# Local and pooled attention before an MLP: value chunks loaded in order and attended as they land

## The chip, the cores and the metric

One core of a Trainium2 chip runs the whole program. The metric is device time in microseconds (us). The kernel before takes 307.57 us, the median of three runs (307.49, 307.57, 308.89). Engines are named as the profile names them: PE (TensorE, matrix multiplication; PEld is its weight load), ACT (ScalarE), DVE (VectorE), POOL (GpSimd) and SP (SyncE, which here only issues loads and stores).

## What is computed

```python
def _attn_ref(q, k, v):
    # q, k, v: 8 batches, 8 heads, 576 tokens, head size 64
    q_d, k_d, v_d = means of q, k, v over groups of 4 tokens
    out_up = repeat(softmax(scale * q_d @ k_d.T) @ v_d, 4)
    mask = abs(i - j) < 4
    out_local = softmax(where(mask, scale * q @ k.T, -1e9)) @ v
    return out_up + out_local

def _moe_ref(x, w_in, w_out):
    # x: 4608 tokens x 512, w_in: 512 x 2048, w_out: 2048 x 512
    h = x @ w_in
    g = h * (1.0 / (1.0 + exp(-1.702 * h)))
    return g @ w_out
```

The attention's output, heads side by side, is the x of the second part. All inputs and the output are float32; the kernel computes its products in bfloat16.

## The kernel before, in words

**Two parts.** Attention runs batch by batch, the MLP by groups of 512 tokens (`n_groups` is 9, `TG` 512). A group's first product (`mm1`, L753, matmuls by `hps_mm` L738) goes through ScalarE's Silu (L749) into `gT`; the second (`mm2`, L770, matmuls at L808) is scaled and stored (L783 to L794). Within group g the attention of batch g+1 is placed between matmuls of `mm1` and `mm2` by a list of positions (`POS`, `POS_G`, L838, L839): a position counts matmul steps, and positions from 16 on are steps of `mm2`. `VDP_0` (L840) is the position at which batch 1's values are pooled by PE.

**Order by hand.** No scheduler orders the instructions: each engine runs its own in the order of the program's text. Only semaphores join engines, and an instruction that waits holds back everything behind it on its engine.

**Batch 0** has no MLP work to hide under; lines 847 to 938 are its order.

- Loads of k, q and w go through POOL's queue and are cast to bfloat16 on the way (`load_1` L183, `load_vb` L214, `load_w_in` L237, `load_w_out` L246). A "quad" (qd) is four heads: q and k come in one load per quad, 128 partitions by 1152 values. POOL's queue holds at most eight loads that have not landed.
- Values come in five chunks of 128 rows that overlap (`KSTART`, steps of 114 tokens), each chunk in two loads of 64 partitions. Before, chunk 4 of batch 0 is asked for first of all, as float32 through SP and ACT (`load_v` at L847, L203), and cast by ACT (`prep_v`, L865, L325). Chunks 0 to 3 come through POOL's queue behind k and q.
- DVE transposes k and q (L261) and sums them over four tokens (`reduce_qk` L304; POOL does the second quad's q by `pool_qk`, L315 and L319). PE makes the masked local scores (`scores` L419: L381 and L394) and the pooled ones (`scores_d` L428: L411); ACT takes their exponentials (L477, L483) into `es` and `ed`.
- `prep_vd_pe` (L351) sums values over four tokens on PE with a selection matrix (L362), in three blocks: kc 0 reads chunks 0 and 1, kc 1 reads 1, 2 and 3, kc 2 reads 3 and 4. ACT copies the blocks to `vd` (L371).
- `av_local0` (L493, L499) multiplies local weights by values for a pair of heads (hp, 0 to 3), `av_down0` (L507, L513 and L522) the pooled ones. Both write to the pair's accumulator `o[hp]`, in which one column of each block of 65 is the sum of weights. Columns 0 to 3 of the blocks belong to chunks 0 to 3, 4 and 5 to chunk 4 and the pooled part, 6 to the pooled part.
- `normalise0` (L537) divides on DVE: a reciprocal (L541) and products (L544, L549), in the parts "a" (blocks 0 to 3), "b" (4 to 6) or both.
- `transp_sum` (L557, L564 and L575; called by `turned`) turns a pair's result so that the model dimension is on partitions, and ACT copies it to `xT` (L587, L591).
- `part` is group 0's first product, started on each quarter of the model dimension as its `xT` comes.
- `warm` (L603, matmuls at L606) issues matmuls that nobody reads; with `z=wf` they are float32 and take two passes.

Before, PE waits until chunks 0 to 3 are there, pools blocks kc 0 and 1, does the local part of pairs 0 and 1 with all five chunks, and DVE normalises part "a".

Of the kernel before, what the change touches and what calls it, by code (L numbers as in the profile page):

```python
# [19 lines left out]
def kernel(  # L20
# [9 lines left out]
    nc = tc.nc  # L30
    B, H, S, D = q.shape
    SD = S // 4
    HP = H // 2
    NQ = H // 4
# [158 lines left out]
        load_1("k", k, kf, b, qd)  # L193
        load_1("q", q, qf, b, qd)

    def load_v(b, gate=None, chunks=range(5), queues=(nc.sync, nc.sync)):
        t = ldp.tile([128, 5, H, D], FP32, name="vf", tag="vf")
        vf[b] = t
        if gate is not None:
            gate(t[0:1, 0, 0, 0:1])  # L200
        for i in chunks:
            for par in range(2):
                queues[par].dma_start(  # L203
                    out=t[64 * par : 64 * par + 64, i],
                    in_=bass.AP(
                        tensor=v.tensor,
                        offset=v[b, 0].offset + (114 * i + KSTART[par]) * D,
                        ap=[[D, 64], [S * D, H], [1, D]],
                    ),
                )  # L210
# [95 lines left out]
                axis=mybir.AxisListType.X, op=ALU.add,  # L306
            )

    def pool_qk(b, qd, names="kq"):
        for name, src in (("k", kT), ("q", qT)):  # L310
            if name not in names:
                continue
            sv = src[b, qd].rearrange("p (j f) a -> p j f a", f=4)
            t1 = work.tile([128, SD, 2, 2], FP32, name="pq", tag="pq")
            nc.gpsimd.tensor_tensor(  # L315
                out=t1, in0=sv[:, :, 0:2, :], in1=sv[:, :, 2:4, :], op=ALU.add
            )
            dst = kdT[qd][:, 0:SD, :] if name == "k" else new_qdT(b, qd)
            nc.gpsimd.tensor_tensor(  # L319
                out=dst, in0=t1[:, :, 0, :], in1=t1[:, :, 1, :], op=ALU.add  # L320
            )
# [26 lines left out]
    def flat(p):  # L348
        return p.rearrange("p x n -> p (x n)")

    def prep_vd_pe(b, pv, kcs=range(3), between=None):  # L351
        n = HP
        vb, vd = vbs[b % 2], vds[b % 2]
        for kc, iis in ((0, (0, 1)), (1, (1, 2, 3)), (2, (3, 4))):
            if kc not in kcs:
                continue
            c0 = 256 * (kc - kcs[0])
            if between and kc == 1:
                between()
            for i in iis:  # L360
                for j in range(2):
                    nc.tensor.matmul(  # L362
                        pv[64 * j : 64 * j + 64, c0 : c0 + D * n],
                        lhsT=psel[:, PSEL.index((i, kc)), :],
                        rhs=sub(
                            vb[:, i], 65 * (2 * j if b else j), (4 * 65, NQ), (65 * (1 if b else 2), 2), (1, D)
                        ),
                        start=(i == iis[0]), stop=(i == iis[-1]),
                        tile_position=(0, 64 * j),
                    )  # L370
        nc.scalar.copy(  # L371
            out=vd[:, kcs[0] : kcs[-1] + 1, :, 0:D],
            in_=pv[:, 0 : 256 * len(kcs)].rearrange(
                "p (k h d) -> p k h d", k=len(kcs), h=HP
            ),
        )


    def bar_others(sp):
# [157 lines left out]
    def normalise0(o, y, u, parts="ab"):  # L537
        yl, yd, rc = y
        ov = o[:, :, 0:455].rearrange("p x (c e) -> p x c e", e=65)
        c0, c1 = {"a": (0, 4), "b": (4, 7), "ab": (0, 7)}[parts]  # L540
        nc.vector.reciprocal(rc[:, :, c0:c1], ov[:, :, c0:c1, 64:65])  # L541
        if "b" in parts:
            st = 2 - u
            nc.vector.tensor_tensor(  # L544
                out=yd.rearrange("p s x d -> p x s d"), in0=ov[:, :, 4 + u : 7 : st, 0:D],
                in1=rc[:, :, 4 + u : 7 : st].to_broadcast([128, 2, 2, D]), op=ALU.mult,
            )
            c1 = 6
        nc.vector.tensor_tensor(  # L549
            out=yl[:, :, c0:c1], in0=ov[:, :, c0:c1, 0:D],  # L550
            in1=rc[:, :, c0:c1].to_broadcast([128, 2, c1 - c0, D]), op=ALU.mult,
        )
# [217 lines left out]
    def mm2(g, gT, steps):  # L770
# [29 lines left out]
        for t, ffc, run in order:  # L800
            if g == n_groups - 1 and t == 3:
                continue
            for f in steps.get(n, ()):
                f()
            n += 1
            if ffc % run == 0:
                ops[t] = pm_tile()
            nc.tensor.matmul(  # L808
                ops[t],
                lhsT=gT[:, ffc, t * 128 : (t + 1) * 128],  # L810
                rhs=w_out_bf[:, ffc, :],
                start=(ffc % run == 0), stop=(ffc % run == run - 1),
            )
            if ffc == n_ffc - 1:
                store(t, ops[t], 0, d_model, nc.scalar, nc.sync, part.get(t))
            elif ffc % run == run - 1:
                keep(t, ops[t])

# [17 lines left out]
            f()  # L836

    POS = [13, 16, 34, 44, 58, 65]  # L838
    POS_G = {0: [16, 18, 29, 42, 56, 65], 1: [13, 16, 35, 44, 58, 65]}  # L839
    VDP_0 = 34  # L840

    o, y, x = {}, {}, {}

    def after(src, eng):
        return lambda t: eng.tensor_copy(out=t, in_=src)

    load_v(0, chunks=[4], queues=(nc.sync, nc.scalar))  # L847
    nc.scalar.preload_act_table_set("exp_and_others")
    load_qk(0, 0)
    load_1("k", k, kf, 0, 1)  # L850
# [1 line left out]
    load_1("q", q, qf, 0, 1)  # L852
    iota_psel()
    fill()
    for i in range(4):
        load_vb(0, i)
    load_w_in(0, 512)
    warm(3, z=wf)
    warm(5, 256)
    make_off()  # L860
    make_ident(di)
    make_psel()
    make_bias()
    end_psel()
    prep_v(0, nc.scalar, 4)  # L865
    prep_1("k", 0, 0)
    prep_1("q", 0, 0)
    sp = scores(0, 0, PA[0:2])
# [2 lines left out]
    prep_1("k", 0, 1)  # L871
    prep_1("q", 0, 1)
    reduce_qk(0, 0, "q")
    pool_qk(0, 1, "q")
    reduce_qk(0, 1, "k")
    for c in range(1, 4):
        load_w_in(512 * c, 512)
    for qd in range(NQ):
        load_qk(1, qd)
    load_w_out(0)  # L880
    load_w_out(4)
    warm(2, z=wf)
    sp = scores(0, 1, PA[0:2])
    exp_local(1, sp)
# [1 line left out]
    for hp in range(4):  # L886
        o[hp] = PA[hp % 3]
        y[hp] = y_tiles0()
    warm(1, z=wf)
    prep_vd_pe(0, PM[0], range(0, 2))  # L890
    for hp in range(2):
        av_local0(hp, o[hp], range(5))
        normalise0(o[hp], y[hp], hp % 2, "a")
    prep_vd_pe(0, PM[1], range(2, 3))
    exp_down(1, scores_d(0, 1, PA[2]))
    nc.scalar.preload_act_table_set("silu_and_others")
    for hp in range(2):
        if hp == 1:
            warm(1, t=PM[0])
        av_down0(hp, o[hp])  # L900
        normalise0(o[hp], y[hp], hp % 2, "b")

    gT0 = new_gT()
    acc = PM + [PA[n][:, u, :] for n in (1, 2, 0) for u in range(2)]
# [4 lines left out]
            for ffc in ffcs:  # L909
                hps_mm(0, ffc, dmc, acc[ffc])  # L910

    def av_whole0(hp):
        av_local0(hp, o[hp], range(5))
        av_down0(hp, o[hp])
        normalise0(o[hp], y[hp], hp % 2)

    def turned(hp, n):
        x = PM if n is None else [PA[n][:, u, :] for u in range(2)]
        transp_sum(y[hp], x)
        copy_x(0, hp, PM if n is None else PA[n][:, :, 0:288])  # L920

    av_whole0(2)
    warm(1, t=PM[0])
    turned(0, None)
    av_whole0(3)
    turned(1, 1)
    part((0, 1), 0)
    part((0, 1), 1)
# [11 lines left out]
    for g in range(n_groups):  # L940
        b = g + 1
        if g == 0:
            load_vb(1, 0)
            load_vb(1, 1)
            prep_qk(1, 0)
            pool_qk(1, 0)
            prep_qk(1, 1)
            load_vb(1, 2)
            load_vb(1, 3)
            load_vb(1, 4)  # L950
            load_w_out(8)
            load_w_out(12, 2)
            load_w_out(14, 2)
            reduce_qk(1, 1, "q")
            reduce_qk(1, 1, "k")
            for qd in range(NQ):
                load_qk(2, qd)
            nc.gpsimd.memset(v4[32:64], 0.0)
            for x, c in ((0, 1.0), (1, 4.0)):
                nc.vector.memset(ones[:, x, :], c)  # L960
            load_v(2, gate=after(w_out_bf[0:1, 14, 0:1], nc.gpsimd))
            load_v4(2)
        elif b == 2:
            for p in (0, 64):
                nc.vector.tensor_copy(out=mask[p : p + 64, 1], in_=mask[64 - p : 128 - p, 0])
            prep_qk(b, 0)
            pool_qk(b, 0)
            prep_qk(b, 1)
            keep_odd(b, 1)
            swap_even("k", b, 1)  # L970
            swap_odd("k", b, 1)
            reduce_qk(b, 1, "k")
            swap_even("q", b, 1)
            swap_odd("q", b, 1)
            load_qk(b + 1, 0)
            prep_vx(b)
            load_v(b + 1)
            prep_v4(b, nc.gpsimd, (0,))
            pool_qk(b, 1, "q")
            prep_v4(b, nc.gpsimd, (1, 2))  # L980
            load_qk(b + 1, 1)
        elif b < B:
            if b + 1 < B:
                load_v(b + 1)
            swap_odd("k", b, 0)
            swap_even("q", b, 0)
            swap_odd("q", b, 0)
            if b > 3:
                prep_v4(b, nc.gpsimd, (0, 1))
            pool_qk(b, 0)  # L990
            prep_qk(b, 1)
            keep_odd(b, 1)
            for name in "kq":
                swap_even(name, b, 1)
                swap_odd(name, b, 1)
            prep_v4(b, nc.gpsimd, (2,) if b > 3 else (0, 1))
            pool_qk(b, 1)
            if b == 3:
                prep_v4(b, nc.gpsimd, (2,))
# [57 lines left out]
```

## Time and profile before

| What | Value |
|---|---|
| Median of three runs | 307.57 us |
| Profiled execution, its own time | 308.58 us |
| Its span, first to last instruction | 306.8 us |
| Time around the span | 1.78 us |
| Instructions | 8494 |
| Mean granted PE clock | 0.999 |
| DMA | 40.01 MB, mean 130 GB/s |
| POOL's queue (q0) | 18352 packets, 14.81 MB |
| Instruction queue (q8) | 28 packets, 0.46 MB |

How to read it: the page gives each engine's busy time; the busy times by stretch say in which part of the span an engine is full; the chain that ended last is followed back from the last instruction, so that its rows are the work that set the time; the timeline lists instructions in order with the idle time before each and what ended it ("<-DMA" is a load, "<-issue" is a wait for nothing that the profile shows). Besides, the trace records when each load's semaphore was raised, by each of the 16 DMA engines that share a load, and when the blocks of program text on the instruction queue were moved.

### The profile page before, as it was taken

How to read it: one execution, taken by the hardware profiler on the slowest of the kernel's cores; microseconds unless marked ns; L12 is line 12 of the kernel's file. 1: busy time of each engine (PE TensorE's matmuls, PEld its weight loads, DVE VectorE, ACT ScalarE, POOL GpSimd, SP SyncE). 2: the span in 40 equal slices, each digit the busy share in tenths (PEclk: the TensorE clock that was granted, in tenths of full speed). 3: DMA queues.
4: the chain of work that ended last, by engine and by line, in shares of the span. 5: the costliest groups of instructions: out<-in, count | busy, mean ns of one | idle time of the engine just before them, and what ended most of it. 6: DMA issues, size and time to landing. Idle time of an engine off the chain costs nothing.

```text
span 306.8 us, 8494 instructions
## 1 busy us (share of the span) xinstructions
PE 298.0 (97%) x3551; PEld 147.8 (48%) x3551; DVE 187.1 (61%) x354; ACT 212.9 (69%) x351; POOL 178.9 (58%) x217
## 2 busy tenths in 40 slices
PE   7879999999999999999999999999999999999995
PEld 3455455444554455445544554455444544444444
DVE  6865523966999689886897689777975430000000
ACT  5545887867887788668966896689769876226511
POOL 8855792599698968976797669845983300000000
PEclk9999999999999999999999999999999999999999
DMA  7999999999899969826973598425101110010012
GB/s 147 152 203 209 173 132 213 177 221 215 177 230 188 188 133 226 219 46 113 232 211 66 88 218 232 84 77 150 72 0 37 36 71 0 34 71 34 0 68 71
DMA packets 64662, 40.01 MB, mean 130 GB/s; under 512 B 44656, under 2 KB 56048, under 8 KB 64624
## 3 DMA queue, kind: packets, MB, share of 16 engines
q0 software_dynamic: 18352, 14.81, 35.8%
q1 hardware_dynamic: 45600, 24.46, 32.3%
q8 instruction: 28, 0.46, 0.6%
q10 hardware_dynamic: 672, 0.20, 0.3%
q14 instruction: 10, 0.08, 0.1%
HBM read 44.83 MB, written 9.44 MB: 177 GB/s over the span
## 4 chain that ended last, share of the span: by engine, by line
PE 93%; DMA 4%; issue 1%; POOL 1%; DVE 0%; ACT 0%; POOLq 0%; DVEq 0%
PE pm L808 40%; PE pm L738 36%; PE pa L681 5%; PE pa L738 5%; DMA qb<-in_q_dram 2%; DMA vb<-in_v_dram 2%; PE pa L449 2%; PE pm L824 1%; PE pa L458 1%; PE pa L394 1%; PE pa L411 0%; POOL kb L183 0%; PE pa L513 0%; PE pa L362 0%; PE pa L499 0%
## 5 line engine op out<-in xcount | busy, mean ns | idle before, releaser
L808 PE MATMUL pm<-w_out_bf,gT 128*128 128x512 bf16 x560 | 126.2, 379 | 0.0
L738 PE MATMUL pm<-xT,w_in_bf 128*128 128x512 bf16 x512 | 119.2, 379 | 0.3 <-ACT xT L591 0.3
L749 ACT ACTIVATE gT<-pm 128x512 bf16<-128x512 f32 x128 | 76.3, 598 | 42.7 <-PE pm L738 42.7
L738 PEld LDWEIGHTS <-w_in_bf 128*128 128x128 bf16 x576 | 55.6, 98 | 67.2 <-issue 0.6
L808 PEld LDWEIGHTS <-gT 128*128 128x128 bf16 x560 | 52.9, 98 | 62.2 <-issue 0.4
L699 DVE TENSOR_TENSOR xT<-pa,r 128x300 bf16<-128x300 f32 (+3 forms) x112 | 28.0, 303 | 18.6 <-ACT r L694 17.8
L787 ACT ACTIVATE osb<-pm 128x512 f32<-128x512 f32 (+2 forms) x37 | 21.5, 580 | 24.1 <-PE pm L808 21.3
L708 POOL TENSOR_TENSOR xT<-xT,ydt 128x576 bf16<-128x576 bf16 x14 | 16.2, 1173 | 31.1 <-DVE xT L699 31.1
L789 DVE TENSOR_SCALAR osb<-pm 128x128 f32<-128x128 f32 x1 | 0.3, 292 | 55.5 <-ACT osb L787 55.5
L491 DVE TENSOR_TENSOR es<-es,mask 128x600 bf16<-128x600 bf16 x28 | 19.0, 708 | 21.2 <-ACT es L477 20.9
L693 ACT ACTIVATE r<-pa 128x504 f32<-128x504 f32 (+1 forms) x42 | 24.0, 571 | 8.4 <-PE pa L681 8.4
L694 ACT ACTIVATE r<-r 128x504 f32<-128x504 f32 (+1 forms) x42 | 25.9, 616 | 1.3
L339 POOL TENSOR_TENSOR v<-v 112x512 f32<-112x512 f32 x18 | 23.5, 1306 | 0.4
L277 DVE TENSOR_REDUCE kT<-kT 32x576 bf16<-32x576 bf16 x22 | 17.5, 795 | 8.7 <-POOL odd L272 8.3
L261 DVE STREAM_TRANSPOSE kT<-kb 128x576 f32<-128x576 f32 x16 | 20.0, 1252 | 3.4 <-DMA kb<-in_k_dram 3.1
L477 ACT ACTIVATE es<-pa 128x600 bf16<-128x600 f32 x32 | 19.7, 668 | 3.4 <-PE pa L394 3.2
L261 DVE STREAM_TRANSPOSE qT<-qb 128x576 f32<-128x576 f32 x16 | 19.8, 1238 | 0.7 <-DMA qb<-in_q_dram 0.3
L738 PE MATMUL pa<-xT,w_in_bf 128*128 128x512 bf16 x64 | 20.0, 379 | 0.0
L315 POOL TENSOR_TENSOR pq<-qT 128x576 f32<-128x576 bf16 x14 | 16.0, 1145 | 6.8 <-DVE qT L277 6.6
L277 DVE TENSOR_REDUCE kT<-odd 32x576 bf16<-32x576 bf16 x22 | 17.5, 795 | 0.7
L277 DVE TENSOR_REDUCE qT<-qT 32x576 bf16<-32x576 bf16 x22 | 17.5, 795 | 0.7
L277 DVE TENSOR_REDUCE qT<-odd 32x576 bf16<-32x576 bf16 x22 | 17.4, 791 | 0.7
(107 smaller groups left out, 344.2 us busy)
## 6 DMA issues: line engine op xcount, KB each, us to landing
out_dram<-osb SPq DMA_DIRECT2D x35, 256.0 KB, 3.2
vf<-in_v_dram SPq DMA_DIRECT2D x61, 128.0 KB, 4.3
v<-in_v_dram SPq DMA_DIRECT2D x72, 96.0 KB, 4.2
kb<-in_k_dram POOLq DMA_DIRECT2D x16, 288.0 KB, 7.1
qb<-in_q_dram POOLq DMA_DIRECT2D x16, 288.0 KB, 9.4
w_in_bf<-in_moe_w_in_dram POOLq DMA_DIRECT2D x4, 512.0 KB, 7.5
w_out_bf<-in_moe_w_out_dram POOLq DMA_DIRECT2D x3, 512.0 KB, 15.6
vb<-in_v_dram POOLq DMA_DIRECT2D x18, 64.0 KB, 6.3
```

What stands on the lines that cost most here:

```text
L261: nc.vector.transpose(out=t32.rearrange("p (i c) -> p c i", c=18), in_=store[b, qd].bitcast(FP32).rearrange("p (c d) -> p c d", c=18),)
L277: nc.vector.tensor_reduce(out=dst, in_=src[:, :, None], axis=mybir.AxisListType.X, op=ALU.add)
L339: eng.tensor_tensor(out=t1[0:112], in0=x[:, :, 0:2, :], in1=x[:, :, 2:4, :], op=ALU.add)
L477: nc.scalar.activation(out=es[2 * qd + u][:, :, 0:300], in_=sp[u][:, :, 0:300], func=AF.Exp, scale=inv_sqrt_d,)
L491: nc.vector.tensor_tensor(out=ev, in0=ev, in1=mask, op=ALU.mult)
L693: nc.scalar.activation(out=r, in_=den, func=AF.Ln)
L694: nc.scalar.activation(out=r, in_=r, func=AF.Exp, scale=-1.0)
L699: nc.vector.tensor_tensor(out=sub(x[u], t0 + at, (114, n), (1, c)), in0=sub(src, c0, (60, n), (1, c)), in1=sub(rc, c0, (60, n), (1, c)), o ...
L738: nc.tensor.matmul(acc, lhsT=w_in_bf[:, dmc, ffc * 128 : (ffc + 1) * 128], rhs=xT[dmc][:, g * TG : g * TG + TG], start=(dmc == 0), stop=(d ...
L749: nc.scalar.activation(out=gT[:, ffc, :], in_=acc, func=AF.Silu, scale=GELU_SCALE)
L787: eng.activation(out=osb, in_=ap, func=AF.Copy, scale=1.0 / GELU_SCALE)
L808: nc.tensor.matmul(ops[t], lhsT=gT[:, ffc, t * 128 : (t + 1) * 128], rhs=w_out_bf[:, ffc, :], start=(ffc % run == 0), stop=(ffc % run == r ...
```

## The change

- The early float32 loads of chunk 4 and ACT's cast go; chunk 4 comes through POOL's queue behind chunk 3, ten loads of values in a row.
- The first block of `w_in` is asked for between POOL's two additions of the second quad's pooled q (`between` in `pool_qk`), not ahead of them.
- `w_out` rows 4 to 7 are asked for after the first two loads of batch 1's values, not before them.
- Pairs 0 and 1 attend in pieces: chunks 0 and 1, then 2, then 3, then 4. `normalise0` gets the parts "p" (blocks 0 and 1) and "q" (2 and 3), so that blocks are divided in three parts. The pooling of values is cut likewise (`psum_v`, `copy_vd`): kc 0 after chunks 0 and 1, kc 1 in two halves around chunk 3, kc 2 after chunk 4; ACT makes three copies in place of two.
- Pair 2's local part stands ahead of the pooled part of pairs 0 and 1, its pooled part right after it.
- Fillers: five of 256 columns become four of 320; one float32 filler of 512 columns becomes two of 256, with the first pieces between them; the two bfloat16 fillers ahead of and after pair 2 go.
- In group 0, `VDP_0` goes from 34 to 36, two positions of `POS_G` from 42 and 56 to 43 and 57, and the first finished store (token tile 0) is scaled by DVE instead of ACT.

```diff
+    def psum_v(b, kc, iis, p, ends=(True, True)):
+        vb = vbs[b % 2]
+        for i in iis:
+            for j in range(2):
+                nc.tensor.matmul(
+                    p[64 * j : 64 * j + 64],
...
+    def copy_vd(b, kcs, pv):
+        nc.scalar.copy(
+            out=vds[b % 2][:, kcs[0] : kcs[-1] + 1, :, 0:D],
...
-        c0, c1 = {"a": (0, 4), "b": (4, 7), "ab": (0, 7)}[parts]
+        c0, c1 = {"a": (0, 4), "b": (4, 7), "ab": (0, 7), "p": (0, 2), "q": (2, 4)}[parts]
...
+                eng = nc.vector if (g, t) == (0, 0) else nc.scalar
+                store(t, ops[t], 0, d_model, eng, nc.sync, part.get(t))
...
-    POS_G = {0: [16, 18, 29, 42, 56, 65], 1: [13, 16, 35, 44, 58, 65]}
-    VDP_0 = 34
+    POS_G = {0: [16, 18, 29, 43, 57, 65], 1: [13, 16, 35, 44, 58, 65]}
+    VDP_0 = 36
...
-    load_v(0, chunks=[4], queues=(nc.sync, nc.scalar))
...
-    for i in range(4):
+    for i in range(5):
         load_vb(0, i)
-    load_w_in(0, 512)
     warm(3, z=wf)
-    warm(5, 256)
+    warm(4, 320)
...
-    prep_v(0, nc.scalar, 4)
...
-    pool_qk(0, 1, "q")
+    pool_qk(0, 1, "q", between=lambda: load_w_in(0, 512))
...
-    load_w_out(4)
...
-    warm(1, z=wf)
-    prep_vd_pe(0, PM[0], range(0, 2))
+    warm(1, 256, z=wf)
     for hp in range(2):
-        av_local0(hp, o[hp], range(5))
-        normalise0(o[hp], y[hp], hp % 2, "a")
-    prep_vd_pe(0, PM[1], range(2, 3))
+        av_local0(hp, o[hp], (0, 1))
+        normalise0(o[hp], y[hp], hp % 2, "p")
+    psum_v(0, 0, (0, 1), PM[1][:, 0:256])
+    copy_vd(0, (0,), PM[1][:, 0:256])
+    warm(1, 256, t=PM[0], z=wf)
+    psum_v(0, 1, (1, 2), PM[0][:, 0:256], (True, False))
     exp_down(1, scores_d(0, 1, PA[2]))
+    for hp in range(2):
+        av_local0(hp, o[hp], (2,))
+    for hp in range(2):
+        av_local0(hp, o[hp], (3,))
+        normalise0(o[hp], y[hp], hp % 2, "q")
+    psum_v(0, 1, (3,), PM[0][:, 0:256], (False, True))
+    copy_vd(0, (1,), PM[0][:, 0:256])
+    for hp in range(2):
+        av_local0(hp, o[hp], (4,))
+    psum_v(0, 2, (3, 4), PM[1][:, 256:512])
+    copy_vd(0, (2,), PM[1][:, 256:512])
     nc.scalar.preload_act_table_set("silu_and_others")
+    av_local0(2, o[2], range(5))
     for hp in range(2):
-        if hp == 1:
-            warm(1, t=PM[0])
         av_down0(hp, o[hp])
         normalise0(o[hp], y[hp], hp % 2, "b")
+    av_down0(2, o[2])
+    normalise0(o[2], y[2], 0)
...
-    av_whole0(2)
-    warm(1, t=PM[0])
     turned(0, None)
-    av_whole0(3)
+    av_local0(3, o[3], range(5))
+    av_down0(3, o[3])
+    normalise0(o[3], y[3], 1)
...
             load_vb(1, 0)
+            load_w_out(4)
             load_vb(1, 1)
```

## The prediction, made before the changed kernel was run

> **What bounds the kernel now.** I read the page first, then busy time by stretches, the chain of waits of the first 30 us, the timeline of the same stretch, and the trace's record of each load's completion.
>
> ```profile
> PE 298.0 (97%) x3551; PEld 147.8 (48%) x3551; DVE 187.1 (61%) x354; ACT 212.9 (69%) x351; POOL 178.9 (58%) x217
> ```
>
> TensorE is busy 97%. By stretches (columns: length, then busy time of PE and the others):
>
> ```profile
> 5.30:16.08 10.78, 8.75 (x214) 5.00 (x212) 8.29 (x7) 6.70 (x15) 9.88 (x14) 1.00 2.00 169
> 16.08:26.44 10.36, 8.78 (x213) 5.90 (x214) 6.39 (x16) 5.24 (x9) 4.91 (x9) 1.00 1.21 206
> 26.44:39.60 13.16, 13.16 (x165) 6.33 (x162) 7.79 (x8) 9.96 (x19) 9.53 (x14) 1.00 1.70 175
> 39.60:58.15 18.55, 18.53 (x346) 9.58 (x335) 8.57 (x28) 16.33 (x26) 9.11 (x11) 1.00 1.14 176
> 58.15:290.00 231.85, 231.85 (x2552) 111.99 (x2552) 152.92 (x270) 170.39 (x277) 141.48 (x156) 1.00 0.55 124
> ```
>
> From 26.44 on PE has no hole. I call 26.44 the dense point: the time follows it one for one, unless the dense part gets new holes. Busy PE before it is partly fillers, so the chain (start, length, what) tells more:
>
> ```profile
> 3.87 6.09 DMA qb<-in_q_dram
> 9.96 0.28 issue
> 10.24 5.79 DMA vb<-in_v_dram
> 16.04 0.04 issue
> 16.08 0.30 PE pm L362 x2
> ...
> 17.06 0.70 DVE yl L549
> 17.76 0.04 issue
> 17.80 0.36 PE pa L513 x6
> ...
> 20.40 0.13 PE pm L575 x3
> 20.53 1.22 issue
> 21.75 0.33 PE pm L575 x5
> ```
>
> The reader is to see three things. The start hangs on value chunk 3, whose load is the twelfth on POOL's queue, could be issued only when the fourth (q's second half) had landed at 9.96, and landed at 16.04. Then VectorE's norm of four columns stands between PE's steps. Then comes 1.22 us of "issue", a hole in PE that no engine and no load ended.
>
> **Completions on POOL's queue** (trace): q and k at 5.53, 7.10, 8.52, 9.96; the eight half chunks of v at 10.94, 11.52, 12.16, 12.78, 13.38, 14.91, 15.56, 16.04; w_in blocks 17.73, 20.25, 23.13, 25.67; next k, q 27.09 to 31.29; w_out 33.85 and 36.92. Fifteen of the sixteen engines' parts of the last three half chunks were there at 13.97, 14.62, 15.08: one engine ran 0.95 late after a 16384-byte block on the "instruction" queue at 11.71 that took 1.74. Half chunks follow each other by 0.6. Load n starts 0.28 after load n-8 has landed.
>
> **Step 1, nothing ahead of k and q.** Two plain loads of 128 KB and ScalarE's 0.61 cast (L325) go. The first k packet came at 3.19, while later k loads that found the queue empty had theirs 1.27 after issue (issue 170.91, packet 172.18), which would be 2.51 here; from 3 to 4 us 43 k packets moved, later 94 in a us. So k and q land between 0 and 0.95 earlier; I take 0.75, near the count of packets. VectorE set-up ends at 5.30, so its first transpose starts at 5.31, not 5.55, and q's follows after 1.14 (its rows overlap by 0.12) at 6.45, not 7.12: 0.65 gained, up to the scores and exps of both quads. The cast lay beside VectorE's transposes and gives nothing itself. Fillers of five by 256 or four by 320 are 1280 columns alike.
>
> **Step 2, values in order.** Chunk 4 comes as two more loads at the end: issues of 0.69 at 10.45 and 11.15 (waits: v's first two half chunks, 10.19 and 10.77 with the 0.75 taken off, plus 0.28). At the pace of 0.6 the last half lands at 16.04 - 0.75 + 1.2 = 16.5, or 0.95 less if the late engine has caught up; bounds 15.5 and 17.4. Chunk 3 lands at 15.3.
>
> **Step 3, pieces.** The scores of quad 0 end 0.65 earlier and the filler is 0.56 instead of 1.12 (the two passes at 13.46, halved), so PE starts on values at 13.4, chunks 0 and 1 having landed at 12.0. Sixteen L499 (0.25), four pooling matmuls (0.3), filler 0.55, four more 0.3, the 24 L411 (0.58): done by 15.5, about when chunk 3 lands; POOL's pooled q, now behind a w_in issue of 0.8, comes at 14.5 and is covered. VectorE's norms of two columns: 0.2 + 0.41 each (0.41 is L549 on 256 elements), the first pair 13.7 to 14.9, the second 15.6 to 16.8. In the new order PE's chunk 4 matmuls wait for these (write after read in the same accumulator) and for chunk 4 itself: 16.85. Four pooling matmuls (0.42 with their latency, as at 16.81) and ScalarE's copy of 256 columns (0.38): 17.75. av_down0 of pair 0 can end then, as before (17.80 to 18.36). So pieces by themselves win only 0.2 here; VectorE's norm that held PE at 17.80 is gone, and chunk 4 takes its place.
>
> **Step 4, what goes between 17.8 and turned(0).** Pair 2's local part (0.34) is now done under ScalarE's copy, and both fillers (0.39 each) are out. VectorE's last norm of pair 0 takes 0.98 from 18.3 to 19.28 as before. turned(0) runs 19.0 to 19.65; without the hole the old one would end 20.86.
>
> **Step 5, the hole.** Counting instructions in both orders, the hole is at PE's row 682 of 7083 in the old order. [...] I cost the hole at nothing left; bounds are 0 and 1.9 (nothing earlier: 21.5 against 19.6). [...]
>
> From turned(0)'s end PE needs 4.52 to the dense run (22.08 to 26.60): 19.65 + 4.52 = 24.2. Pair 2's norm ends 21.6, pair 3's 23.2, each 0.5 ahead of need. Head: 26.6 - 24.2 = **2.4 gained**.
>
> **Step 6, the weights.** All weights now stand behind two more half chunks: 1.2 later less 0.75 at the front, and w_in's first block is issued at 13.0 after a POOL add instead of 11.22: w_in's stream starts at 14.3, not 13.5, so +0.8. w_in has slack of microseconds. w_out rows 4 to 7 moved past two half chunks more: 33.85 + 0.8 + 1.2 + 2.6 (the spacing of w_in blocks) = 38.5, needed four matmuls after mm2's first at 39.60, that is at 40.5 less the gain. w_out's last block landed at 48.58, then 49.2, needed at 51.25 less the gain. Both allow about 2.0. Batch 1's last chunk, 42.2 then 43.2, is needed at 45.4 plus 0.43 (VDP_0 two steps later): covered. So of 2.4, 2.0 remain, and I take off 0.2 for the many steps with margins under 0.3: **1.8**.
>
> **At nothing:** the first store moves ScalarE's 0.60 to VectorE between 52.3 and 53.5, where VectorE waited 1.22; POS_G shifts attention by one matmul (0.22), and batch 1's x is ready at 57.83 against 59.02 for its first reader there. If that cover failed it would cost at most these 0.22.
>
> **Sum.** The profiled execution took 308.58, span 306.8 and 1.78 around it: 305.0 + 1.78 = 306.8. It lies 1.01 above the median of the three runs, 307.57; the same shift there gives **305.8**.
>
> **Rivals.** A, the forecast: 305.2 to 306.4, chance 0.50. F, chunk 4 without the late engine: 0.9 more in the head, and weights that land 0.7 earlier with it: 304.9, chance 0.13. C, k and q gain nothing or the block lands on chunk 4: chunk 4 at 17.4, 0.9 less of 2.4, and a little of it lost again at w_out: 306.5, chance 0.15; for it speaks the late engine of before. B, the hole stays or moves (only a guess names its cause): turned(0) ends between 20.9 and 22.08: 306.4 to 307.57, centre 307.2, chance 0.15. E, slower: PE has little to do from 15.5 to 16.9 and falls to half pace. Its first L606 passes started 0.85 apart (2.75, 3.60, 4.45), later ones 0.43 (9.73, 10.16), and it needed from 1.73 to about 6, though the clock column reads full there. Two such stretches of 4.3 in the dense part lose 2.15 each: 4.3 - 1.8 gives 310.1; it turns slower than before from 3.6 us of dense work at half pace. Against it: holes of 0.82 and 1.22 changed nothing, and fillers stand between. Chance 0.07. [...]
>
> About 0.5%, 1.54 us, is what a measurement of this kernel can tell from no change. Faster by more (under 306.03): 0.37 of A, all F, 0.02 of C: 0.52. Slower: E, 0.07. Same: 0.41. The range 304.9 to 307.5 leaves out E, some of B and some of F.
>
> **What would show it.** First transpose at 5.3 and q's at 6.45; chunk 4's L499 near 16.85; no PE "issue" over 0.5 between 19 and 22; L738 without holes from about 24.2; no wait at L808's fifth matmul. A late chunk 4, a hole that stays, or a wait for w_out would make it wrong.

## The result and the profile after

The changed kernel takes **311.76 us**, the median of 13 executions (310.08 to 313.57); the kernel before, run beside it, 308.89 (13 executions, 307.49 to 310.26). The ratio is **1.009**, 95% interval 1.0062 to 1.0119: slower by 2.8 us, where it was forecast to be 1.8 faster. The profiled execution of the changed kernel is the fastest of its 13: 310.08, span 308.3, against 308.58 and 306.8 before. So the profile shows only 1.5 of the 2.8; the rest has to be looked for in the other executions (e12 to e16 below). Ratios here and below leave out the few executions that took over 1.5% more than the fastest of their kernel, among them one of e17 that took 1078.28.

The page after, busy time and then the chain's shares by engine (before, the chain's share was 93% PE and 4% DMA):

```profile
PE 298.9 (97%) x3550; PEld 148.0 (48%) x3550; DVE 189.1 (61%) x359; ACT 212.0 (69%) x350; POOL 180.8 (59%) x219
...
PE 81%; DMA 13%; POOL 3%; ACT 1%; issue 1%; DVE 0%; POOLq 0%
```

PE is as busy as before, so busy time tells nothing. The chain does: 13% of it now runs over loads. Its rows from q's load on, after (start, length, what):

```profile
3.87 6.70 DMA qb<-in_q_dram
10.57 0.28 issue
10.86 0.68 POOL vb L214
...
13.03 1.15 POOL pq L315
14.18 0.75 POOL w_in_bf L237
14.92 0.02 issue
14.94 0.68 POOL qdT L321
15.62 1.45 POOL w_in_bf L237 x2
17.07 11.66 DMA w_in_bf<-in_moe_w_in_dram
28.73 0.28 issue
29.02 12.09 DMA w_out_bf<-in_moe_w_out_dram
41.11 0.28 issue
...
43.53 8.67 DMA w_out_bf<-in_moe_w_out_dram
52.20 0.04 issue
52.24 0.81 PE pm L808 x3
```

Before, the chain left the loads at 16.08 and stayed on engines. Now it goes through POOL's queue to 52.20: q's second half lands, the last values are issued, a POOL addition (L315) stands ahead of w_in's first block and another (L321) ahead of the other three, each later load waits for one to land, and the last block of w_out is what PE waits for. The busy times by stretch, after, with the columns of before's table (the third stretch begins at 26.50 here):

```profile
5.30:16.08 10.78, 9.12 (x229) 5.27 (x229) 9.67 (x12) 6.55 (x15) 9.55 (x14) 1.00 1.82 131
16.08:26.44 10.36, 9.13 (x201) 6.13 (x201) 5.82 (x16) 5.21 (x9) 5.67 (x10) 1.00 1.19 186
26.50:39.60 13.10, 13.10 (x162) 6.25 (x161) 7.79 (x8) 9.90 (x19) 8.86 (x13) 1.00 1.31 201
39.60:58.15 18.55, 17.40 (x329) 9.05 (x328) 7.88 (x26) 14.41 (x24) 10.68 (x13) 1.00 1.59 172
```

Two things are to be seen. In the last column the first stretch moved 131 GB/s where before had 169, the second 186 for 206: 38 x 10.78 and 20 x 10.36 are 617 KB less by 26.44, some 3 us of the load stream at its 200. The trace's records of packets place it: from 14 to 17 us POOL's queue moved 64, 18 and 107 KB in each us, before 177, 199 and 181, because w_in's first packet came at 15.65, not at 12.96. And in the fourth stretch PE is busy 17.40 of 18.55; before it was 18.53. The holes there, from PE's timeline after:

```profile
41.15 2.10 PE L808 MATMUL pm<-w_out_bf,gT 128*128 128x512 bf16 x9 [0.75 <-DMA w_out_bf<-in_moe_w_out_dram]
...
52.24 0.81 PE L808 MATMUL pm<-w_out_bf,gT 128*128 128x512 bf16 x3 [0.29 <-DMA w_out_bf<-in_moe_w_out_dram]
```

Counted from the start of one matmul to the start of the next the two gaps are 1.13 and 0.67, with a third of 0.48 at 57.58 that ACT's scaling of a store (osb, L787) ended. A matmul's own step is 0.22, so the three gaps hold 1.6 of idle time. Group 0's second product began 0.24 earlier (39.36 against 39.60), so the head won 0.24 of the 2.4 forecast; group 1's first L738 began 1.34 later (59.49 against 58.15), and the last matmul of all is 1.34 later too. All that this execution lost, it lost inside group 0's second product.

### The profile page after: what moved, and what is told of

It reads as the page before. It is cut to its first block, busy times and chain, and to the rows that moved or that the text cites. A ratio compares the mean times of both kernels' runs of the same rounds, so it can differ in the third digit from the quotient of the medians.

```text
span 308.3 us, 8492 instructions
## 1 busy us (share of the span) xinstructions
PE 298.9 (97%) x3550; PEld 148.0 (48%) x3550; DVE 189.1 (61%) x359; ACT 212.0 (69%) x350; POOL 180.8 (59%) x219
## 4 chain that ended last, share of the span: by engine, by line
PE 81%; DMA 13%; POOL 3%; ACT 1%; issue 1%; DVE 0%; POOLq 0%
PE pm L808 36%; PE pm L738 34%; DMA w_out_bf<-in_moe_w_out_dram 7%; PE pa L681 4%; DMA w_in_bf<-in_moe_w_in_dram 4%; PE pa L738 2%; DMA qb<-in_q_dram 2%; PE pa L449 2%; PE pm L825 1%; POOL vb L214 1%; PE pa L458 1%; POOL w_in_bf L237 1%; POOL w_out_bf L246 0%; ACT r L694 0%; POOL kb L183 0%
## 5 line engine op out<-in xcount | busy, mean ns | idle before, releaser
L738 PE MATMUL pm<-xT,w_in_bf 128*128 128x512 bf16 x512 | 119.2, 380 | 0.3 <-ACT xT L591 0.3
L738 PEld LDWEIGHTS <-w_in_bf 128*128 128x128 bf16 x576 | 55.5, 98 | 67.2 <-issue 0.6
L787 ACT ACTIVATE osb<-pm 128x512 f32<-128x512 f32 (+2 forms) x36 | 20.9, 579 | 23.8 <-PE pm L808 21.1
L789 DVE TENSOR_SCALAR osb<-pm 128x512 f32<-128x512 f32 (+1 forms) x2 | 1.0, 487 | 55.5 <-ACT osb L787 55.5
L738 PE MATMUL pa<-xT,w_in_bf 128*128 128x512 bf16 x64 | 20.0, 379 | 0.0
L315 POOL TENSOR_TENSOR pq<-qT 128x576 f32<-128x576 bf16 x14 | 16.0, 1145 | 6.1 <-DVE qT L277 5.9
L214 POOL DMA_DIRECT2D vb<-in_v_dram x20 | 13.7, 698 | 7.3 <-DMA w_in_bf<-in_moe_w_in_dram 3.1
```

The source lines that it names most:

```text
L738: nc.tensor.matmul(acc, lhsT=w_in_bf[:, dmc, ffc * 128 : (ffc + 1) * 128], rhs=xT[dmc][:, g * TG : g * TG + TG], start=(dmc == 0), stop=(d ...
L787: eng.activation(out=osb, in_=ap, func=AF.Copy, scale=1.0 / GELU_SCALE)
```

## The experiments

Ratios are to the kernel before, run beside each, with 95% intervals; 0.1% is 0.31 us. A diff is against the changed kernel unless it says otherwise. Of each execution the mean granted clock is known; one stretch of 3.4 us at half clock makes it 0.994 or 0.995 (0.995 in the profiles of e1 and e4), and two of them would, by an estimate from the same count, make it 0.989. Of the changed kernel 9 of 13 executions lie under 0.996, of the kernel before 20 of 145.

**e3 and e4, loads and pieces apart.** e3 is the changed kernel with all loads as before; e4 is the kernel before with the changed kernel's loads alone. e3's edit (e4's is its reverse, made to the kernel before):

```diff
+    load_v(0, chunks=[4], queues=(nc.sync, nc.scalar))
...
-    for i in range(5):
+    for i in range(4):
         load_vb(0, i)
+    load_w_in(0, 512)
...
+    prep_v(0, nc.scalar, 4)
...
-    pool_qk(0, 1, "q", between=lambda: load_w_in(0, 512))
+    pool_qk(0, 1, "q")
...
+    load_w_out(4)
...
-            load_w_out(4)
```

> The changed kernel with all its loads as before: chunk 4 early in float32 with ScalarE's cast, w_in's first block behind chunk 3, w_out rows 4 to 7 ahead of batch 1's values. Pieces, positions and the store stay as changed. Theory W: weights land as in the kernel before, no wait for w_out; the dense point at 26.2 or earlier; as fast as before or up to 0.5 faster. Theory P: slower than before by 1 or more, with a late dense point. Theory O: slower by 1 or more with holes in the second product of group 0 at the moved positions.

> The kernel before with only the loads of the change: chunk 4 last on POOL's queue, w_in's first block between POOL's additions, w_out rows 4 to 7 behind two loads of batch 1's values. It attends in whole as before, with its fillers and positions. Theory W: weights 3 to 4 us late as in the changed kernel, waits for w_out of about 1 us in all, dense point not earlier than before: slower than before by 1.5 to 3. Theory P or O: within 0.5 of before.

e3: 1.0008 (0.9979 to 1.0037), and no wait for w_out. e4: 1.0076 (1.0044 to 1.0107). The loads alone make nearly the whole loss, the pieces alone neither loss nor gain. Of e4's executions 9 of 12 lie under a mean clock of 0.996, of e3's 3 of 12: e4 came to half clock without pieces. e4's profile shows what late rows 4 to 7 of w_out can do when the head does win: its second product began at 38.39, the rows landed at 42.48. PE's timeline of e4, then its busy times in two stretches around the wait (columns as above; the last three numbers are the granted clock, the DMA share and GB/s):

```profile
38.39 1.04 PE L810 MATMUL pm<-w_out_bf,gT 128*128 128x512 bf16 x4
42.52 3.50 PE L810 MATMUL pm<-w_out_bf,gT 128*128 128x512 bf16 x9 [3.09 <-DMA w_out_bf<-in_moe_w_out_dram]
```

```profile
38.60:42.00 3.40, 0.83 (x4) 0.29 (x3) 1.99 (x5) 2.14 (x4) 2.35 (x4) 0.99 2.43 154
42.00:45.40 3.40, 2.88 (x7) 0.99 (x7) 0.00 (x0) 0.60 (x1) 2.64 (x4) 0.50 1.63 75
```

Nine matmuls take 3.50, where the changed kernel's nine take 2.10: this wait cost its length, 3.09, and then half the clock for 3.4 us more. PE was busy 0.83 of the 3.40 ahead.

**e1, e2 and e8, one postponed load at a time.** e1 puts rows 4 to 7 of w_out back ahead of batch 1's values, e2 puts w_in's first block right behind the ten value loads, e8 does both.

```diff
     load_w_out(0)
+    load_w_out(4)
...
             load_vb(1, 0)
-            load_w_out(4)
```

```diff
     for i in range(5):
         load_vb(0, i)
+    load_w_in(0, 512)
...
-    pool_qk(0, 1, "q", between=lambda: load_w_in(0, 512))
+    pool_qk(0, 1, "q")
```

> The changed kernel with one edit: w_out rows 4 to 7 are asked for ahead of batch 1's first two value loads again. Theory W (the loss is PE waiting for w_out in the second product of group 0, because everything on POOL's queue lands some 3.5 us later): rows 4 to 7 land about 1.2 earlier, near 39.9, ahead of their need at 40.2, so the first wait (0.9) goes; the last block of w_out stays at about 52.2 and its wait of 0.45 stays; about 0.9 better than the changed kernel, still 1.5 to 2 slower than before. Theory P (the pieces cost the time): no change from the changed kernel. Theory O (the shifted positions and the store on VectorE cost it): no change either.

> The changed kernel with one edit: the first block of w_in is asked for right behind the ten value loads, ahead of POOL's addition, as the kernel before had it. Theory W, with the hole of the load stream at 15 to 17 us as its main cause: the block is issued at about 13.0, not 14.1, every weight lands about 1.1 earlier, w_out rows 4 to 7 near 40.0 and the last block near 51.1, both about when they are needed: 1 to 1.5 better than the changed kernel, 1 to 2 slower than before at most. If two more value loads on a slow stream are the main cause, the gain is under 0.5. Theory P or O: no change from the changed kernel.

> The changed kernel with both weight orders of before: w_in's first block right behind the ten value loads, w_out rows 4 to 7 ahead of batch 1's values. Theory W: rows 4 to 7 land near 38.8, the last block near 51; no wait at the fifth matmul, at most 0.3 later: 2 to 2.5 better than the changed kernel, within 0.5 of before. Theory P or O: still 1 or more slower than before.

e1: 1.007 (1.0045 to 1.0096); e2: 1.0047 (1.002 to 1.0075); e8: 1.0044 (1.0013 to 1.0076). By the ratios w_in's place is worth most, though the intervals overlap; the two together give back half of the loss, not the whole that e8's expectation gave. In e8 PE still has gaps of 0.51 for rows 4 to 7 and 1.56 for the last block, which landed at 52.25 after all.

e1's profile brought something else. Its stretches before and after 21.50, and then a stretch of the same length in the kernel before:

```profile
18.10:21.50 3.40, 2.64 (x69) 1.75 (x69) 1.73 (x7) 2.22 (x4) 2.76 (x5) 1.00 1.05 155
21.50:24.90 3.40, 3.40 (x56) 2.56 (x57) 3.29 (x10) 0.94 (x3) 0.41 (x1) 0.50 1.21 197
```

```profile
19.00:22.40 3.40, 2.18 (x76) 1.59 (x76) 2.77 (x8) 1.40 (x3) 0.81 (x2) 1.00 1.24 207
```

From 21.5 to 24.9 PE ran at half clock, and its second product began at 40.88, 1.5 after the changed kernel's. No wait like e4's 3.09 stood ahead of it: PE was busy 2.64 of 3.40, more than the 2.18 at which the kernel before kept its full clock. So neither a long wait nor busy time says when this happens here.

The traces narrow it down. In e10 these stretches begin at 19.91, 60.87 and 313.45, that is 40.96 and 252.58 apart: 12.0 and 74.0 steps of 3.413 us. In the profiles of the kernel before and of the changed one the full clock lasted 300.37 and 303.79, 88.0 and 89.0 such steps. Count each matmul by its columns times the share that it uses of 128 by 128, the largest form in the traces; some sixteen full ones of 512 columns, 8192 in this count, fill a step (in the dense part they start 0.216 apart). Of all steps at full clock between 7 and 75 us in the 19 profiles, the four with the least work are the four that half clock followed: some 880 and 1990 in e10, 1670 in e4, 2080 in e1. The next one, 2220 in the changed kernel, kept its clock; counted by where matmuls start and not where they end, the changed kernel's least step has 2060. The local matmuls (L499) use 64 by 64, a quarter of the largest form, so they count for little. This is a reading of few steps, with a distance between 2080 and 2220 that is no larger than what the way of counting moves, and no run varied it: what decides it stays open.

**e5 and e6, the hole and the small edits.** e5 is the kernel before with 32 more instructions on PE (16 matmuls of 8 columns, each with its weight load) ahead of the first local scores, where PE waits for q: any edge between two blocks of the program's text falls 32 instructions earlier in PE's work; e6 is the kernel before with the changed positions and the first store on DVE.

```diff
     warm(5, 256)
+    warm(16, 8)
```

```diff
+                eng = nc.vector if (g, t) == (0, 0) else nc.scalar
...
-    POS_G = {0: [16, 18, 29, 42, 56, 65], 1: [13, 16, 35, 44, 58, 65]}
-    VDP_0 = 34
+    POS_G = {0: [16, 18, 29, 43, 57, 65], 1: [13, 16, 35, 44, 58, 65]}
+    VDP_0 = 36
```

> [...] Theory T (the 1.22 hole is PE waiting for its next block of program text): the edge before it is passed ahead of the wait for chunk 3, the second text block moves at 17 to 18, not 19.48, the hole at the turning matmul of pair 0 goes or shrinks under 0.4, and the kernel is 0.5 to 1.2 faster than before. Rival H (the hole belongs to that matmul's data): the hole stays at the same matmul with 1.1 to 1.3; time as before or up to 0.4 slower.

> The kernel before with only the shifted positions of group 0 (VDP_0 36, 43 and 57) and the first store's scaling on VectorE. Theory W: within 0.5 of before; a hole of about 0.3 at the end of group 0's second product, as at 57.58 in the changed kernel and at 57.19 in the run with old loads, so 0.2 slower. Theory O: slower by 1 or more.

e5: 1.0012 (0.9984 to 1.0039); the hole at L575 is gone, but PE has another, also ended by nothing:

```profile
15.39 1.02 PE L606 MATMUL pm<-wf 128*128 128x512 f32 x2 [1.03 <-issue]
```

The hole stands at another instruction with 32 more ahead of it, and taking it from its place gains nothing by itself; the expected 0.5 to 1.2 did not come. e6: 1.0012 (0.9977 to 1.0047), with the hole still ending at 21.73 (0.74) and a new gap of 0.49 at 56.44, 0.27 more than a matmul's step, ended by ACT's osb (L787). A gap of 0.48 or 0.49 there is in all ten profiles with the changed positions and store and the old order of the second product, and in none of the six with the old positions. The time alone can't tell it from nothing.

**e7, e9, e10 and e11, attempts at a better version.** e7 is the kernel before with chunk 4 last on POOL's queue and nothing else changed. e9 is e7, e10 is e8, and e11 is the kernel before, each with an order of the second product that needs the later rows of w_out later.

```diff
-    load_v(0, chunks=[4], queues=(nc.sync, nc.scalar))
...
-    for i in range(4):
+    for i in range(5):
         load_vb(0, i)
...
-    prep_v(0, nc.scalar, 4)
```

```diff
-                      (0, 2), (0, 3), (1, 2), (1, 3), (2, 2), (2, 3), (3, 2), (3, 3))
+                      (0, 2), (1, 2), (0, 3), (1, 3), (2, 2), (2, 3), (3, 2), (3, 3))
```

> The kernel before with only one thing of the change: chunk 4 comes last on POOL's queue and not early in float32; w_in's first block is asked for right behind it, w_out and the attending stay as before. Theory W with the order of the queue as its cause: weights about 1.2 to 1.5 late (two half chunks of 0.6), no wait for w_out over 0.5; within 0.7 of before, and faster by up to 1 if the second text block comes early as in the run with new loads and whole attending (there at 17.15, with mm2's first matmul at 38.39 against 39.60). Theory P has nothing to say here. If q's last load again lands later (10.4 to 10.8 against 9.96) though nothing is ahead of it, the early loads did not delay k and q.

> The kernel before with chunk 4 last on POOL's queue (as in the run of that alone) and one more edit: in group 0's second product token tiles 0 and 1 take w_out rows 8 to 11 both before either takes rows 12 to 15, so that the last block of w_out is needed four matmuls and one attention step (some 1.9 us) later. Theory W: in the run of chunk 4 alone the head was 1.9 earlier (mm2's first matmul at 37.72 against 39.60) and 1.1 to 1.4 of it was lost at that block (landed 50.97); without that wait 1 to 1.9 faster than before. If the time stays as before, the weights were not what took the gain back.

> The changed kernel with both weight orders of before and the same later need of w_out's last block. Theory W: the wait of 1.3 to 1.6 at that block goes; with the pieces' later head (mm2 first at 39.2 and not 37.7) within 0.5 of before. Against the run of chunk 4 last with the same later need it shows what the pieces themselves cost: by the holes on VectorE's norms (0.6 and 0.3) and the copy of three blocks 0.8 to 1.4 slower than that. If pieces cost nothing, the two are equal.

> The kernel before with only the later need of w_out's last block. Theory W: the kernel before has 1 to 2.6 us to spare there (landed 48.58 to 49.9, needed at 51.2), so nothing changes: within 0.3 of before. If it is faster by 0.5 or more, the kernel before waits for w_out in most of its executions too.

e7: 1.0014 (0.9985 to 1.0043), so moving chunk 4 to the end costs little; the other two postponements, which e4 has besides, cost the 0.6% between them. In e7's profile the second product began at 37.72, 1.88 earlier than before, and PE then waited 1.06 for the last block of w_out (landed 50.97). e9: 1.0056 (1.0033 to 1.0078), e10: 1.0195 (1.0175 to 1.0214), e11: 1.0028 (1.0006 to 1.0049). None of the three swaps did what was expected. The swapped order finishes two token tiles close together, and what scales them stands on its engine behind the attention: PE waited 1.42 in e9 and 1.62 in e11 for ACT's osb (L787), and 4.08 in e10 for DVE's (L789), after which it ran at half clock again. e9 also waited 1.42 for w_out's rows 4 to 7, which landed at 40.93. e10's stretches around its wait:

```profile
57.50:60.90 3.40, 0.40 (x2) 0.19 (x2) 3.26 (x9) 1.99 (x3) 0.00 (x0) 1.00 0.96 167
60.90:64.30 3.40, 3.40 (x9) 1.22 (x8) 3.37 (x5) 0.52 (x1) 0.00 (x0) 0.50 1.00 195
```

e11 has the same program as the kernel before up to 39 us, yet its profile has no hole at L575 and its second product began at 38.02, not 39.60.

**e12, e13 and e15, without the wait for w_out.** The changed kernel (e12), the kernel before (e13) and e7 (e15) with group 0's second product reading only rows 0 to 3 of w_out; this part of the output is not the reference's.

```diff
-                rhs=w_out_bf[:, ffc, :],
+                rhs=w_out_bf[:, ffc if g else ffc % 4, :],
```

> The changed kernel, but group 0's second product reads only w_out's rows 0 to 3 (512 of 2048 hidden rows, four times over), so that it never waits for later weights; group 0's output is not the reference's. Its pair is the kernel before with the same edit. Theory W alone (late weights are the whole loss): as fast as its pair or up to 0.5 faster. If half-clock stretches of PE or the pieces cost time beside the weights, it stays 0.5 to 1.5 slower than its pair.

> The kernel before with the same edit: group 0's second product reads only rows 0 to 3 of w_out. Theory W: the kernel before hardly waits for weights, so within 0.4 of before.

> The kernel before with chunk 4 last on POOL's queue, attending in whole, and group 0's second product reading only rows 0 to 3 of w_out. Theory W: the earlier head of that order (up to 1.9 in one profile) is now not given back: 0.7 to 1.8 faster than the kernel before with the same reading. If it is equal to that, the earlier head was an accident of one execution.

e12: 1.0043 (1.0012 to 1.0073); e13: 0.9973 (0.9948 to 0.9999); e15: 1.0008 (0.998 to 1.0036). The wait is worth some 0.47% of the changed kernel. The same edit gave the kernel before 0.27%, at the edge of what such runs tell, though its profile shows no such wait; 0.7% between e12 and e13 is not w_out. e15 stays 0.35% over e13. Its second product began at 39.89, with the hole at L575 there (1.18), where e7 had no hole and 37.72: the early start of e7 does not come with its order of loads in every execution. Of e12's executions 6 of 12 lie under a mean clock of 0.996, at a median of 310.84 against 309.27 for the other six: 1.6 us, near half of 3.4. Of e13's none do. In e12's profile, one at full clock, PE waits for batch 1's values instead (0.57 at 45.76, a gap of 0.84).

**e14 and e16, more fillers.** Two calls of fillers, three matmuls in all, go where the pieces leave PE idle; e16 adds the edit of e12 to them (group 0's second product reads rows 0 to 3 alone).

```diff
     copy_vd(0, (1,), PM[0][:, 0:256])
+    warm(2, 256, t=PM[1], z=wf)
...
     av_down0(2, o[2])
+    warm(1, 256, t=PM[0][:, 256:512])
     normalise0(o[2], y[2], 0)
```

> The changed kernel with three more fillers on PE: two float32 ones of 256 columns while it waits for VectorE's norms ahead of chunk 4, a bfloat16 one ahead of the turning of pair 0. Rival K (PE falls to half clock in many executions, since the pieces leave it idle): mean granted clocks under 0.996 become rare (they were seen in 9 of 13 executions of the changed kernel, 10 of 87 of the kernel before), and the time comes 1 or more closer to before. Theory W: clocks may recover, but the time stays within 0.7 of the changed kernel, since the weights come when they come.

> The changed kernel with two more fillers (two float32 matmuls of 256 columns ahead of the chunk 4 matmuls, one of 256 columns ahead of the first turn) and with group 0's second product reading only rows 0 to 3 of w_out, so that its output is not the reference's. Theory (late weights and half pace are together the whole loss): the two gains add, 1.009 less 0.0035 less 0.0047, so 0.998 to 1.002, and close to the kernel before with the same edit (0.9973); hardly an execution under a mean clock of 0.996. Rival (one cause hides the other, the gains do not add, or a third cause is left, such as the late values of batch 1): 1.003 to 1.006.

e14: 1.0055 (1.0028 to 1.0083), 310.33 us at the median, 1.1 us less than the changed kernel by the ratios, with more work on PE; 1 of 12 executions lies under 0.996, where it was 9 of 13. PE still waits 1.52 at 41.47 for rows 4 to 7. The intervals of e14 and the changed kernel overlap, so the 0.35% is likely and not settled; that the fillers keep the clock up is plain from the counts. e16: 1.0007 (0.9983 to 1.0031), 1 of 12 under 0.996: the two gains, 0.47% and 0.35%, add up to 0.83%. The 0.34% left between e16 and e13 is at the edge of what such runs tell. In e16's profile the head has won nothing (second product at 39.96), and PE waits 0.16 and 0.21 for batch 1's values.

**e17, old loads, pieces and fillers.** e3 with the two fillers.

> All loads as in the kernel before, with the pieces, the positions, the store of the changed one and the two more fillers. Theory (pieces alone, at full pace, win about what the head's start moves): the same loads with pieces and no more fillers gave 1.0008, a quarter of its executions under a mean clock of 0.996; with the fillers 0.997 to 1.001. Rival (the fillers stand on the path, since chunk 4 is there early with the old loads and the pieces wait for VectorE's norms alone): 1.001 to 1.004. Under 0.998 it would be the fastest of all kernels that compute the reference.

1.0018 (0.999 to 1.0046): no gain, by e3's measure perhaps a loss of 0.1%. None of the versions that compute the reference beats the kernel before; e3, e5, e6, e7 and e17 can't be told from it.

## Why the prediction was wrong

**Step 6 failed, and the gain that was to stand against it did not come.** It put w_in 0.8 later; measured, w_in's first block landed 3.58 later (21.31 for 17.73), rows 4 to 7 of w_out 4.19 (41.11; forecast 38.5) and the last block 3.62 (52.20; forecast 49.2). So the two came 2.6 and 3.0 after their forecasts, more than the allowance of "about 2.0", and PE waited for both although the head had won only 0.24. The mechanism stood in the step; its terms were too small. The first block of w_in was issued at 14.12, not 13.0, because the value loads ahead of it wait for q's second half, and that came at 10.57, not at 9.96 less 0.75. Its first packet came 1.53 after the issue (15.65), where the step used 1.3, from loads of k. And the step took w_in's delay from the start of its stream alone: while w_in moved from 12.96 on before, the last values went beside it, and the two together filled the queue; after, the values end at 15.8 and w_in starts from nothing. Part of this is the one profile of before, which was early: in the six others with the early loads w_in's first block landed at 17.72 to 18.55, rows 4 to 7 at 37.27 to 38.23 (four profiles record them) and the last block at 49.49 to 50.78, so against their middle the changed kernel is 3.2, 3.1 and 2.0 later. The loads by themselves (e4) cost 0.76%. This step alone does not settle the sign: without the waits (e12) the changed kernel is still 0.43% slower, and only with the fillers besides (e16) is it level with the kernel before.

**Step 1: right at the first load, nothing at the last.** In the twelve profiles without the early loads the first k lands at 5.33 to 5.70. In six of the seven with them it lands at 6.32 to 6.56, and the seventh is the very profile that the prediction was made from (5.53). q's second half lands at 9.91 to 11.16 (median 10.81) without and at 9.96 to 11.20 (median 11.03) with them. The saving of nearly 1 us at the first load is 0.2 at the last, and the profile of before sat at the early end for both.

**Step 2: right.** Chunk 4 landed at 16.33 (forecast 16.5); chunk 3, though, at 15.84, not 15.3.

**Step 3: right in its mechanism, too small in its terms.** PE began on values at 14.18 (forecast 13.4): its pooled scores (L411) at 13.05 wait for DVE's sum, and that stands behind the transpose of the late q. Then comes a hole of 0.40 that no engine and no load ended (steps 4 and 5 have more on it). So the norms of the second pieces came late, and PE waited for both, as PE's timeline after shows:

```profile
14.91 0.19 PE L499 MATMUL pa<-vb,es 64*64 64x65 bf16 x1 [0.40 <-issue]
...
17.95 0.25 PE L499 MATMUL pa<-vb,es 64*64 64x65 bf16 x4 [0.51 <-DVE yl L549]
18.50 0.25 PE L499 MATMUL pa<-vb,es 64*64 64x65 bf16 x4 [0.30 <-DVE yl L549]
```

Forecast for chunk 4's matmuls was 16.85. The copy of the last block ended at 19.51 (forecast 17.75). Chunk 4 had landed 1.6 before its matmuls started: the norms, not the values, are what the pieces wait for. That write after read in the accumulator was named in the step and priced on a start 0.8 too early. Where no hole of PE and no half clock stood ahead, the second product began at 37.72 to 38.52 in the four profiles that attend in whole (e4, e7, e9, e11) and at 38.91 to 39.15 in the three with pieces (e8, e12, e14): there the pieces lose time and win none.

**Steps 4 and 5: the hole went, the gain did not come.** turned(0) began at 20.91 (forecast 19.0); its weight loads have a hole of 0.18 where they had 1.4 and PE 1.22. No run shows step 5's term, a hole that costs nothing. What the runs showed in its place: the second block of program text (16384 bytes on the instruction queue) came at 19.28, hardly earlier than before's 19.48; PE simply reached that row later, 21.52 being 1.3 after the block's end at 20.24; and a hole of 0.40 came ahead of it. The dense point is 26.19 where it was 26.44: 0.25 earlier, and 2.4 was forecast. Over all profiles the block's coming is not fixed by the program: in those with the order of before, the hole at L575 is there when the block came at 19.42 to 19.72 (before, e6, e13, e15) and not when it came at 17.15 to 18.46 (e4, e7, e9, e11). In the four with the hole it ends 1.35 to 1.38 after the block had been moved. The hole of 0.40 in the changed kernel, among the matmuls of chunks 0 and 1, has the same mark: it ends 1.55 after the block at 11.76 (1.60 long). Among the records of PE and its weight load in order of start it is at the 448th in seven profiles (changed, e1, e2, e3, e5, e16, e17), whatever instruction stands there, and the hole at L575 at the 702nd or 703rd, 254 or 255 records further on. In the kernel before the 28 blocks were moved while PE went from its 207th record to its 7073rd; that makes, by estimate, 254 records to a block. So the hole left L575 and a smaller one came one block ahead. What such a hole costs can be seen in the kernels that attend in whole: the second product began at 39.59 to 39.89 in the four profiles with the hole at L575, at 37.72 to 38.52 in the four with none. In these eight profiles late blocks and holes go together; that the one makes the other is a reading, and what sets a block's time is open.

**The rivals.** B came in part: a hole of 0.40 one block ahead took the place of most of the old one, and turned(0) ended at 21.84, inside B's 20.9 to 22.08; but B's times, 306.4 to 307.57, lack the waits for w_out. E, half pace, ended nearest (310.1) and had 0.07. Half clock is there: in 9 of 13 executions, by an estimate from their mean clocks (0.989 to 0.995) for 3.4 or 6.8 us where it assumed 4.3, worth some 1.1 by e14 and 1.6 for a single execution by e12, though in the changed kernel itself the nine had a median of 311.82 and the other four 311.19. It is likely the smaller part of the loss, and it was argued away by holes that had done no harm in one profile. No rival had the weights eating more than the gain; that the two allowances of 2.0 rested on a term worked out from one profile's landings was the place to look for it.

**The size.** The changed kernel's 0.9% is, by cause, 0.47% waits for w_out, about 0.35% half clock, and 0.1% that is not told apart from nothing. Held against e13 in place of the kernel before, 0.34% is left beside these two, so the account is closed only to about that. By edit it is some 0.5% the places of w_in's first block and w_out's rows 4 to 7; chunk 4's place (e7, 0.14%) and the pieces (e3, 0.08%) can't be told from nothing one by one. "At nothing" missed by a little: the shifted positions and the store leave the gap of e6, 0.27 a profile (0.09%), where 0.22 was named as the most.

## What to carry to other kernels

Where loads are issued only when an older one has landed (here 0.28 after it), a load moved later held up those behind it, and compute put ahead of an issue on the same engine counted as part of that delay: w_in's first block landed 3.58 later, w_out's rows 4 to 7 4.19 and its last block 3.62. Price the last load of the queue, not the one that is moved. Work cut into pieces for data that lands late needs the engine between the pieces to keep up: here PE waited 0.51 and 0.30 for DVE's norms, and 9 of 13 executions lie under a mean clock of 0.996, with fillers in such places (e14) 1 of 12. Landings vary by 1 us from execution to execution (q's second half at 9.96 in the kernel before and 11.20 in e11, the same program up to there), so a margin of 2 us worked out from them should be held against at least that.

## What the runs showed of the hardware that was not expected

- PE's clock was halved for stretches of 3.4 us, one or two in a row, after a wait of 3.09 (e4) and one of 4.08 (e10), but also after a stretch with PE busy 2.64 of 3.40 (e1), and in some executions of one kernel and not in others (6 of 12 in e12 lie under a mean clock of 0.996). In e10 these stretches begin 12.0 and 74.0 steps of 3.413 us apart.
- Two loads taken from the very start brought the first k nearly 1 us earlier (5.33 to 5.70 without them; 6.32 to 6.56 with them in six of seven profiles, 5.53 in the seventh) and the fourth load on POOL's queue 0.2 (medians of 10.81 and 11.03).
- A block of program text, 16384 bytes, took 0.88 to 1.92 to move, and the same program got its second block at 17.87 (e11) and at 19.48 (before), or at 15.41 (e12) and at 19.28 (changed).
- The limit of eight loads on POOL's queue goes with the program: its loads raise eight semaphores in turn (99 to 106 in the trace), and a load is issued 0.28 after the load that raised the same one before it has landed. No run shows whether the queue itself would take more.
